# A ring of seven places for the second weight matrix, an earlier read of partial results, and a third inverse class in sixteen frequency classes

## The chip, the cores and the metric

The kernel runs on one core of one Trainium2 chip. Time is device microseconds of one execution. The kernel before takes 1217.4 us (median of three runs, 1216.28 to 1218.68). One of its executions was profiled: it took 1216.67 us, and from its first to its last instruction 1214.9 us.

## The reference

The kernel computes `x + s * g` for `x` of 2048 rows and 1024 columns. `xn` is the layer norm of `x`. `s` is a spectral filter of `xn`: a two-dimensional real Fourier transform, a product with the complex weights `w_r + i w_i`, and the inverse transform. `g` is a feed-forward block with hidden width 3584:

```python
xn = _layernorm(x, axis=-1)
X = rfft2(xn) * (w_r + 1j * w_i)
s = irfft2(X, s=(S, D))
h = silu(xn @ w1)
g = silu(h @ w2)
return x + s * g
```

## The kernel before, in words

**Two streams of work share the engines.** The feed-forward block is the foreground: it gives TensorE (PE in the profile) most of its matmuls. The Fourier transforms are the background: small matmuls that are put between the foreground's, with long chains of additions on VectorE (DVE).

**The second feed-forward matmul** (`h @ w2`) is done as seven products in place of eight, in the manner of Strassen, on sums and differences of blocks. Product `m` (0 to 6) has eight row blocks `j`; I write (4,5) for product 4, row block 5. Each (m,j) is 42 matmuls of 512 columns into one PSUM tile `pb` (lines 563 to 565), in two halves of 21. Each matmul is in half precision, three to one product of 32-bit numbers: high part by high part, high by low, low by high.

**w2 in pieces.** For each product, 14 pieces of w2 (128 by 512) are loaded into a ring of six places (`jr`), by DMAs that GpSimd (POOL) issues (line 421). For products 4 and 5 a piece is the sum of two blocks of w2: a second DMA adds the second block onto the first (line 425, "join"), and must wait until the first has landed. Then ScalarE (ACT) makes the high part (line 244) and VectorE the low part (line 247). `w2_gen` (lines 412 to 464) hands this out in steps: at the step of piece n it issues loads up to n + 5 and joins up to n + 3, and then the high part of piece n. A piece's place in the ring is free when VectorE has made its low part.

**Partial results.** Products 1, 3, 4 and 5 leave partial sums in DRAM (`pd`), through a ring of eight places (`pt`), and products 4 and 6 read them back (`load_parts`, line 552, DMAs of SyncE, SP in the profile). In product 4, VectorE adds the product to both partial results (lines 615 and 616, tiles `pl4_j_1` and `pl4_j_0`); the one is stored again, the other goes through a last chain: SiLU on ScalarE (line 653), the factor from the spectral filter on VectorE (line 641), an accumulating DMA that adds `x` (line 644) and a store (line 645), both issued by GpSimd.

**The inverse transform** goes by four residue classes c of rows, in the order 1, 3, 0, 2. For each class, four groups of matmuls (line 1318, PSUM tile `iu`, groups g = 0 to 3, 48 matmuls each) are followed by additions on VectorE, by `split` (line 1392: `us`, high part on ScalarE, low part on VectorE, line 1395), and then by a second set of matmuls (line 1407, PSUM tile `id`, 48 for each of four parts p), whose every part reads all four `us`. `iu` and `id` share a pool of two PSUM tiles, so the third group waits until VectorE has read the first. There are two forms of the additions: `coarse` (line 1321: eight classes of frequencies, matmuls of 128 columns, 13 VectorE instructions for a group) and `post` (line 1344: sixteen classes, matmuls of 64 columns, 32 VectorE instructions). The tuple `FINE` (line 25) names the classes that use `post`.

**What sets the order.** Nothing is reordered at run time: each engine has one queue in the order in which the program issues. The builder runs through the 56 (m,j); after each half it takes one step of `w2_gen` and as many background steps as its own clock of PE and VectorE allows (`meter` and `work`). More VectorE instructions in a background step therefore move the later background steps to later (m,j). SP's and POOL's DMAs stand in such queues too, and one that waits holds up those behind it.

Of the kernel before, what the change touches and what calls it, by code (L numbers as in the profile page):

```python
# [10 lines left out]
F32 = mybir.dt.float32  # L11
# [10 lines left out]
WARM = [38, 8, 0, 0, 8, 0, 0, 0]  # L22
LEAD, PAUSE, LAST, EARLY = 1.0, -1, 6, 2
IORDER = (1, 3, 0, 2)
FINE = (1, 3)
DIRECT = tuple((6, j) for j in range(8))
SUMMED = (4, 5)
TURNED = (2, 3)
# [88 lines left out]
def spectral_ffn(ctx, tc, x, w_r, w_i, w1, w2, ca, kc, ci, tw, pm, out):  # L117
# [15 lines left out]
    H = {"p": hstack.enter_context(tc.tile_pool(name="hid", bufs=1))}  # L133
    pf = ctx.enter_context(tc.tile_pool(name="pf", bufs=4, space=PSUM))
    pt = ctx.enter_context(tc.tile_pool(name="pt", bufs=2, space=PSUM))
# [59 lines left out]
    def tile_of(pool, shape, dtype, name, tag, bufs):  # L195
        while len(held.get(tag, ())) >= bufs - 1:
            d = held[tag][0]
            deferred.remove(d)
            d[1]()
        return pool.tile(shape, dtype, name=name, tag=tag, bufs=bufs)  # L200
# [211 lines left out]
    def w2_gen():  # L412

        todo = [(m, q) for m in range(7) for q in range(NP)]
        raw = {}

        def load(n):
            if n < len(todo):
                m, q = todo[n]
                raw[n] = J["p"].tile([128, 512], F32, name=f"jr{n}", tag="jr", bufs=6)  # L420
                nc.gpsimd.dma_start(raw[n], ws[m][q] if m in ws else w2_block(m, q, 0))  # L421

        def join(n):
            if n < len(todo) and todo[n][0] in SUMMED:
                nc.gpsimd.dma_start(raw[n], w2_block(*todo[n], 1), accum_op=OP.add)

        def split(n):
            m, q = todo[n]
            if q % 7 == 0:
                w2t[m, q // 7] = fp.tile([128, 7, 2, 512], F16, name=f"w2_{m}_{q // 7}", tag="big", bufs=4)  # L430
            high(w2t[m, q // 7][:, q % 7, 0], raw[n], sc2[:, q:q + 1])

        def rest(n):
            m, q = todo[n]
            w = w2t[m, q // 7][:, q % 7]
            low(w[:, 1], raw.pop(n), sc2[:, q:q + 1], w[:, 0])
            ready2[0] = n

        fed = [0, 0]

        def feed(loads, joins):
            while fed[1] < min(joins, fed[0]):
                join(fed[1])
                fed[1] += 1
            while fed[0] < min(loads, len(todo)):
                load(fed[0])
                fed[0] += 1

        feed(4, 0)
        yield 0  # L450
        yield 0
        for n, (m, q) in enumerate(todo):
            while q % 7 == 0 and (done2[0] < m - 1 or chunks[0] <= (3 if m else q // 7) and m < 2):
                if n and ready2[0] < n - 1:
                    rest(n - 1)
                elif n:
                    feed(min(fed[0] + 1, n + 6), n + 6)
                yield 0
            feed(n + 5, n + 3)
            split(n)  # L460
            if n and ready2[0] < n - 1:
                rest(n - 1)
            yield 0.1
        rest(n)
# [87 lines left out]

    def load_parts(m, j):
        for k in READS[m]:
            t_ = tile_of(H["p"], [128, 512], F32, f"pl{m}_{j}_{k}", "pt", 8)
            nc.sync.dma_start(t_, pd[k, j])
            part[k, j] = t_

# [28 lines left out]
    def acc(m, j, ps, cols=slice(0, 512)):  # L587
        tt = nc.vector.tensor_tensor
        g, p = j // 4, j % 4
        ask_rows(m, j)  # L590

        def fresh(name):
            return tile_of(H["p"], [128, 512], F32, f"{name}_{j}", "pt", 8)

        def keep(k, t_):
            store("pt", 2, lambda: nc.sync.dma_start(pd[k, j], t_))

        def evac():
            if m == 0:
                kept[j] = H["p"].tile([128, 512], F32, name=f"kept{j}", tag="kept", bufs=8)  # L600
                nc.scalar.activation(kept[j], ps, AF.Copy)
            elif m == 1:
                t_ = fresh("c11")
                tt(t_, kept[j], ps, op=OP.subtract)
                keep(0, t_)
            elif m == 2:
                tt(kept[j], kept[j], ps, op=OP.add)
            elif m == 3:
                t_ = fresh("c21")
                nc.scalar.activation(t_, ps, AF.Copy)  # L610
                tt(kept[j], kept[j], ps, op=OP.subtract)
                keep(1, t_)
            elif m == 4:
                t_, u = part.pop((1, j)), part.pop((0, j))
                tt(t_, t_, ps, op=OP.add)
                tt(u, u, ps, op=OP.add)
                keep(0, u)
                return final(2 * g + 1, p, 0, t_)
            elif m == 5:
                t_ = fresh("c12")  # L620
                nc.scalar.activation(t_, ps, AF.Copy)
                tt(kept[j], kept[j], ps, op=OP.add)
                keep(2, t_)
                return final(2 * g + 1, p, 1, kept.pop(j))
            else:
                t_, u = part[2, j][:, cols], part[0, j][:, cols]
                tt(t_, t_, ps, op=OP.subtract)  # L627
                tt(u, u, ps, op=OP.add)
                a_, b_ = final(2 * g, p, 1, t_, cols), final(2 * g, p, 0, u, cols)

                def both():
                    x_, y_ = a_(), b_()
                    return (lambda: (x_ and x_(), y_ and y_(), None)[2]) if x_ or y_ else None

                return both

        return evac
# [27 lines left out]
    A = {}  # L665
# [322 lines left out]
    def open_f():  # L988
        J["p"] = ctx.enter_context(tc.tile_pool(name="jit", bufs=1, side="right"))
        J["i"] = ctx.enter_context(tc.tile_pool(name="fi", bufs=1, side="right"))  # L990
        B["es"] = ExitStack()
        B["p"] = B["es"].enter_context(tc.tile_pool(name="flt", bufs=1, side="right"))
        B["k"], B["v"], B["w"], B["z"] = {}, {}, {}, {}
        B["a"] = J["i"].tile([128, 8192], F16, name="kv", tag="a", bufs=1)
        A["junk"] = J["p"].tile([128, 512], F32, name="junk", tag="jr", bufs=6).bitcast(mybir.dt.bfloat16)

    def f_gen():
        bp = B["p"]
# [298 lines left out]
    def i_gen(c):  # L1297
# [10 lines left out]
        def mat(g):  # L1308
            n_ = 2 if c in FINE else 1
            ps = pt.tile([128, 2, n_, 4, 2, 64 // n_], F32, name=f"iu{c}_{g}", tag="ft")  # L1310
# [210 lines left out]
    with tc.manual_schedule():  # L1521
# [49 lines left out]
        J = {}  # L1571
# [90 lines left out]
        for n, (m, j) in enumerate(seq):  # L1662
# [16 lines left out]
            for k in range(2):  # L1679
                while ready2[0] < m * NP + 7 * k + 6:  # L1680
                    slot(wq)
                if m == 6 and j and k == 0:
                    load_parts(m, j)
                mm2(m, j, ps, k)
                if k == 0:
                    settle()
                    if m < 6 or j == 0:
                        load_parts(m, j)
                    tick()
                    work()  # L1690
# [41 lines left out]
```

## Time and profile before

| What | us |
|---|---|
| median of three runs | 1217.4 |
| the profiled execution | 1216.67 |
| its span, first to last instruction | 1214.9 |
| TensorE matmuls, busy | 1199.7 (99%) |
| VectorE busy | 1024.9 (84%) |
| ScalarE busy | 519.3 (43%) |
| GpSimd busy | 319.6 (26%) |
| moved by DMA | 304.31 MB, 250 GB/s in the mean |

In a timeline row the columns are: start in us from the span's start, length in us, engine, line, operation, out<-in, shapes, count; in brackets the idle time of that engine before it and what ended it. Rows of one kind that follow each other are merged, with a count. `pb`, `iu`, `id`, `jr`, `us` are the tiles named above; the profile leaves out their numbers. A share of busy time is a mean over stages: what a change is worth is read in its own stage, here the last two products but two (about 950 to 1130 us).

### The profile page before, as it was taken

To read this page: it belongs to the slowest core of one execution; us is meant where nothing else is said; L and a number is where in the kernel's file an instruction comes from. 1 tells how busy PE (TensorE), PEld (TensorE's weight loads), DVE (VectorE), ACT (ScalarE), POOL (GpSimd) and SP (SyncE) were. 2 spreads that over 40 slices of the span, in tenths; PEclk is the share of its full clock that TensorE was granted. 3 is DMA by queue.
4 is the path that set the end of the run, shared out by engine and by line. 5 is a ranking of instruction groups with operands and counts; after the bars stand their busy time and mean duration, and the time that the engine had idled before them with its cause. 6 is when DMAs were issued, how large, how long until landed. Compare 5 with 4: busy or idle time off the path is not lost.

```text
span 1214.9 us, 21954 instructions
## 1 busy us (share of the span) xinstructions
PE 1199.7 (99%) x8362; PEld 596.3 (49%) x8362; DVE 1024.9 (84%) x2196; ACT 519.3 (43%) x713; POOL 319.6 (26%) x491
## 2 busy tenths in 40 slices
PE   8999999999999999999999999999999998999998
PEld 5544455445445544544444455444454444554545
DVE  7578889999988999589969999966897896979855
ACT  5874556768557656353624222221222223233112
POOL 2240133334222222233322334620222223221000
PEclk9999999999999999999999999999999999999999
DMA  7478657679589886859898998995988999898798
GB/s 245 135 156 203 186 193 259 198 250 342 161 293 301 270 300 197 256 144 246 253 286 243 253 294 251 242 269 184 220 252 258 259 318 335 268 330 270 244 349 309
DMA packets 166186, 304.31 MB, mean 250 GB/s; under 512 B 31600, under 2 KB 84752, under 8 KB 166080
## 3 DMA queue, kind: packets, MB, share of 16 engines
q1 hardware_dynamic: 125344, 175.61, 46.6%
q0 software_dynamic: 40448, 127.16, 36.3%
q8 instruction: 65, 1.06, 0.3%
q14 instruction: 41, 0.34, 0.1%
q10 hardware_dynamic: 288, 0.13, 0.0%
HBM read 185.92 MB, written 112.74 MB: 246 GB/s over the span
## 4 chain that ended last, share of the span: by engine, by line
PE 89%; DVE 5%; DMA 2%; ACT 2%; issue 1%; POOL 0%; SPq 0%; DVEq 0%; ACTq 0%; POOLq 0%
PE pa L479 44%; PE pb L563 13%; PE pb L565 13%; PE pb L564 13%; PE fx L1034 2%; DMA jr<-in_B_w_dram 2%; PE id L1407 2%; PE iu L1318 1%; ACT xp L742 1%; DMA x<-in_A_x_dram 1%; PE fa L822 1%; PE fa L823 1%; PE fa L824 1%; PE tp L757 0%; DVE w L247 0%
## 5 line engine op out<-in xcount | busy, mean ns | idle before, releaser
L479 PE MATMUL pa<-xnT,w 128*128 128x512 f16 x2688 | 585.5, 379 | 2.3 <-DVE xnT L766 1.1
L479 PEld LDWEIGHTS <-w 128*128 128x128 f16 x2688 | 262.0, 98 | 313.4 <-ACT w L244 3.1
L563 PE MATMUL pb<-w,ht 128*128 128x512 f16 (+2 forms) x812 | 301.0, 372 | 0.0
L564 PE MATMUL pb<-w,ht 128*128 128x512 f16 (+2 forms) x812 | 300.4, 372 | 0.0
L565 PE MATMUL pb<-w,ht 128*128 128x512 f16 (+2 forms) x812 | 300.3, 372 | 0.0
L565 PEld LDWEIGHTS <-ht 128*128 128x128 f16 x812 | 79.5, 98 | 91.3 <-issue 0.3
L563 PEld LDWEIGHTS <-ht 128*128 128x128 f16 x812 | 79.4, 98 | 90.3 <-issue 0.2
L564 PEld LDWEIGHTS <-ht 128*128 128x128 f16 x812 | 79.5, 98 | 87.1
L495 ACT ACTIVATE h<-pa,s 128x512 f32<-128x512 f32 x112 | 75.4, 677 | 62.9 <-PE pa L479 59.0
L244 ACT ACTIVATE w<-jr,sc 128x512 f16<-128x512 f32 x98 | 67.7, 712 | 48.4 <-DMA jr<-in_B_w_dram 30.5
L244 ACT ACTIVATE hosum<-hr,hs 128x1536 f16<-128x1536 f32 x28 | 44.1, 1574 | 97.0 <-DVE hr L524 71.8
L247 DVE SCALAR_TENSOR_TENSOR w<-jr,sc,w 128x512 f16<-128x512 f32 x98 | 71.6, 745 | 3.2 <-ACT w L244 3.2
L517 POOL DMA_DIRECT2D hd_sum<-hosum x26 | 26.1, 1004 | 174.0 <-DVE hosum L247 110.8
L247 DVE SCALAR_TENSOR_TENSOR hoone<-h,hs,hoone 128x2048 f16<-128x2048 f32 x28 | 65.6, 2344 | 6.5 <-ACT hoone L244 6.4
L421 POOL DMA_DIRECT2D jr<-in_B_w_dram x56 | 41.8, 752 | 89.4 <-ACT us L1394 27.8
L244 ACT ACTIVATE hoone<-h,hs 128x2048 f16<-128x2048 f32 x28 | 55.9, 1997 | 15.7 <-DMA hd_one<-hoone 9.1
L247 DVE SCALAR_TENSOR_TENSOR hosum<-hr,hs,hosum 128x1536 f16<-128x1536 f32 x28 | 50.7, 1810 | 5.8 <-ACT hosum L244 5.8
L517 POOL DMA_DIRECT2D hd_one<-hoone x26 | 29.4, 1133 | 88.3 <-DVE hoone L247 56.5
L653 ACT ACTIVATE pl<-pl,c 128x512 f32<-128x512 f32 (+2 forms) x28 | 17.6, 655 | 75.9 <-DVE pl L627 52.3
L523 DVE TENSOR_TENSOR hr<-h 128x1024 f32<-128x1024 f32 x28 | 34.1, 1219 | 17.8 <-ACT h L495 17.6
L244 ACT ACTIVATE w<-w1r,rs 128x1024 f16<-128x1024 f32 x28 | 32.0, 1143 | 38.6 <-DVE w L247 17.4
L1394 ACT ACTIVATE us<-uu 128x1024 f16<-128x1024 f32 x16 | 16.8, 1053 | 62.1 <-DVE uu L234 62.1
(265 smaller groups left out, 1722.3 us busy)
## 6 DMA issues: line engine op xcount, KB each, us to landing
ht<-hd_one SPq DMA_DIRECT2D x64, 448.0 KB, 7.6
hd_one<-hoone POOLq DMA_DIRECT2D x26, 1024.0 KB, 7.6
ht<-hd_sum SPq DMA_DIRECT2D x48, 448.0 KB, 6.3
jr<-in_B_w_dram POOLq DMA_DIRECT2D x84, 256.0 KB, 7.2
hd_sum<-hosum POOLq DMA_DIRECT2D x26, 768.0 KB, 5.7
w1r<-in_B_w_dram SPq DMA_DIRECT2D x28, 512.0 KB, 7.3
w2m<-in_B_w_dram SPq DMA_DIRECT2D x28, 512.0 KB, 6.1
ws<-scr POOLq DMA_DIRECT2D x42, 256.0 KB, 6.2
```

The source lines that it names most:

```text
L244: nc.scalar.activation(hi, raw, AF.Copy, scale=scale)
L247: nc.vector.scalar_tensor_tensor(lo, raw, scale, hi, op0=OP.mult, op1=OP.subtract)
L421: nc.gpsimd.dma_start(raw[n], ws[m][q] if m in ws else w2_block(m, q, 0))
L479: nc.tensor.matmul(ps, w[:, wh, d], xt[:, xh, d], start=(n == 0), stop=(n == 23))
L495: nc.scalar.activation(h32[q, g][:, 2 * (c % 2) + f % 2], ps, AF.Silu, scale=s1[:, f:f + 1])
L517: defer(1, lambda: stores[0].dma_start(hall[names, g][:, :, :, q].rearrange("f k p h s -> f k p (h s)"), o.rearrange("f k p h s -> f k p ( ...
L523: tt(sums[:, 0:2], hq[:, 0::2], hq[:, 1::2], op=OP.subtract)
L563: nc.tensor.matmul(ps, hh[:, 0], w[:, 0], start=first, stop=False)
L564: nc.tensor.matmul(ps, hh[:, 0], w[:, 1], start=False, stop=False)
L565: nc.tensor.matmul(ps, hh[:, 1], w[:, 0], start=False, stop=last)
L1034: nc.tensor.matmul(o, k[rows_, h, e + 2 * x, kh, kind], B["v"][u, h][rows_, e + 2 * x, vh, cols], start=(n == 0 and kind == 1), stop=(n == ...
L1407: nc.tensor.matmul(ps[:, half, g], us[g][rows_, uh, 2 * p + r], C["ci"][rows_, ch, g, r], start=(n == 0 and r == 0), stop=(n == 2 and r == 1))
```

## The change

Three edits, and what follows from them in the sizes of the rings.

1. The ring of w2 pieces has seven places in place of six; at the step of piece n, loads go up to n + 6 and joins up to n + 4.
2. In product 4 the partial results of (4,1) to (4,7) are asked for ahead of the first half's matmuls, as product 6 did already, and not behind them. The ring of partial results gives one place up: seven in place of eight.
3. Class 0, the third of the inverse transform, uses `post` (sixteen classes) in place of `coarse`.

```diff
-FINE = (1, 3)
+FINE = (1, 3, 0)
...
         def load(n):
             if n < len(todo):
                 m, q = todo[n]
-                raw[n] = J["p"].tile([128, 512], F32, name=f"jr{n}", tag="jr", bufs=6)
+                raw[n] = J["p"].tile([128, 512], F32, name=f"jr{n}", tag="jr", bufs=7)
                 nc.gpsimd.dma_start(raw[n], ws[m][q] if m in ws else w2_block(m, q, 0))
...
                 elif n:
-                    feed(min(fed[0] + 1, n + 6), n + 6)
+                    feed(min(fed[0] + 1, n + 7), n + 7)
                 yield 0
-            feed(n + 5, n + 3)
+            feed(n + 6, n + 4)
             split(n)
...
     def load_parts(m, j):
         for k in READS[m]:
-            t_ = tile_of(H["p"], [128, 512], F32, f"pl{m}_{j}_{k}", "pt", 8)
+            t_ = tile_of(H["p"], [128, 512], F32, f"pl{m}_{j}_{k}", "pt", 7)
...
         def fresh(name):
-            return tile_of(H["p"], [128, 512], F32, f"{name}_{j}", "pt", 8)
+            return tile_of(H["p"], [128, 512], F32, f"{name}_{j}", "pt", 7)
...
-                if m == 6 and j and k == 0:
+                if m in (4, 6) and j and k == 0:
                     load_parts(m, j)
                 mm2(m, j, ps, k)
                 if k == 0:
                     settle()
-                    if m < 6 or j == 0:
+                    if m < 4 or m == 5 or j == 0:
                         load_parts(m, j)
```

What this does to the order of the engines' queues is shown at three places. The first is PE, at the third group of class 0 (`iu0_2`); `ht4_5_0` and `ht4_5_1` are the two halves of the operand of (4,5). Before:

```order
L565 LDWEIGHTS ht4_5_0_11178
L565 MATMUL pb4_5_11440<-w2_4_0_9522,ht4_5_0_11178 128x512
L1318 LDWEIGHTS zt0_10704
L1318 MATMUL iu0_2_11475<-tables_8768,zt0_10704 128x128
```

And with the change:

```order
L565 LDWEIGHTS ht4_5_1_11183
L565 MATMUL pb4_5_11462<-w2_4_1_10052,ht4_5_1_11183 128x512
L1318 LDWEIGHTS zt0_10707
L1318 MATMUL iu0_2_11526<-tables_8770,zt0_10707 128x64
```

The third group stood behind the first half of (4,5) and now stands behind the whole of it, and it has 64 columns in place of 128. The first two groups stand where they stood, ahead of (4,5). The fourth group moves from behind (4,5) to behind (4,6), the `id` matmuls of class 0 from the middle of (5,0) and of (5,1) to the middle of (5,2) and of (5,3), the `iu` matmuls of class 2 from behind (5,3) to behind (5,5), and its `id` matmuls from the middle of (5,7) to behind (6,0).

The second place is POOL's queue at the first accumulating DMA of the last chain (`pl4_0_1`). Before:

```order
L425 DMA jr76_10733<-in_B_w_dram 128x512
L421 DMA jr78_11003<-in_B_w_dram 128x512
L644 DMA pl4_0_1_10696<-in_A_x_dram 128x512
L425 DMA jr77_10897<-in_B_w_dram 128x512
L421 DMA jr79_11118<-in_B_w_dram 128x512
L425 DMA jr78_11003<-in_B_w_dram 128x512
L421 DMA jr80_11148<-in_B_w_dram 128x512
L644 DMA pl4_1_1_10891<-in_A_x_dram 128x512
```

And with the change:

```order
L425 DMA jr76_10703<-in_B_w_dram 128x512
L421 DMA jr78_10900<-in_B_w_dram 128x512
L425 DMA jr77_10736<-in_B_w_dram 128x512
L421 DMA jr79_11006<-in_B_w_dram 128x512
L644 DMA pl4_0_1_10699<-in_A_x_dram 128x512
L425 DMA jr78_10900<-in_B_w_dram 128x512
L421 DMA jr80_11121<-in_B_w_dram 128x512
L425 DMA jr79_11006<-in_B_w_dram 128x512
L421 DMA jr81_11151<-in_B_w_dram 128x512
L644 DMA pl4_1_1_10871<-in_A_x_dram 128x512
```

One pair, the join of piece 77 and the load of piece 79, has moved ahead of the accumulating DMA; behind it each join and load is one piece further on.

The third place is VectorE at the end of the additions for the last group of class 0 (`uu0_3`), up to the low part of that group (`us0_3`), which the `id` matmuls of class 0 read. Before:

```order
L234 TENSOR_TENSOR uu0_3_11723<-ub0_3_11713 128x2x128
L641 SCALAR_TENSOR_TENSOR pl4_5_1_11466<-fs3_1_0_11565,s_sc_209,pl4_5_1_11466 128x512
L615 TENSOR_TENSOR pl4_6_1_11673<-pl4_6_1_11673,pb4_6_11647 128x512
L616 TENSOR_TENSOR pl4_6_0_11675<-pl4_6_0_11675,pb4_6_11647 128x512
L1395 SCALAR_TENSOR_TENSOR us0_3_11792<-uu0_3_11723,us0_3_11792 128x1024
```

And with the change:

```order
L234 TENSOR_TENSOR uu0_3_11899<-ub0_3_11870 128x2x128
L247 SCALAR_TENSOR_TENSOR w2_6_0_11829<-jr85_11320,sc2_219,w2_6_0_11829 128x512
L641 SCALAR_TENSOR_TENSOR pl4_7_1_11772<-fs3_3_0_11824,s_sc_209,pl4_7_1_11772 128x512
L622 TENSOR_TENSOR kept0_6696<-kept0_6696,pb5_0_11835 128x512
L247 SCALAR_TENSOR_TENSOR w2_6_0_11829<-jr86_11492,sc2_219,w2_6_0_11829 128x512
L247 SCALAR_TENSOR_TENSOR w2_6_0_11829<-jr87_11522,sc2_219,w2_6_0_11829 128x512
L1395 SCALAR_TENSOR_TENSOR us0_3_11999<-uu0_3_11899,us0_3_11999 128x1024
```

The low part of the last group stood behind the results of (4,6); now it stands behind those of (4,7) and (5,0) and behind four pieces of product 6.

More of the change, by code (lines that the diff above doesn't have):

```diff
@@ L994, in open_f @@
         B["a"] = J["i"].tile([128, 8192], F16, name="kv", tag="a", bufs=1)
-        A["junk"] = J["p"].tile([128, 512], F32, name="junk", tag="jr", bufs=6).bitcast(mybir.dt.bfloat16)
+        A["junk"] = J["p"].tile([128, 512], F32, name="junk", tag="jr", bufs=7).bitcast(mybir.dt.bfloat16)
     def f_gen():
```

## The prediction

> **What bounds the kernel now.** I read the page first (busy times, chain of waits), then the waits of TensorE alone, then the timelines of one engine after the other back from the place that these named. These three rows are from the page's busy times, its chain, and the view of PE's waits:
>
> ```profile
> PE 1199.7 (99%) x8362; PEld 596.3 (49%) x8362; DVE 1024.9 (84%) x2196; ACT 519.3 (43%) x713; POOL 319.6 (26%) x491
> PE 89%; DVE 5%; DMA 2%; ACT 2%; issue 1%; POOL 0%; SPq 0%; DVEq 0%; ACTq 0%; POOLq 0%
> PE iu L1318 <- DVE uw L1329: 4.0, 2, 2.4
> ```
>
> TensorE is the bound: any matmul time that is saved, and any gap that closes, comes off the end, and any gap that opens is added. Its largest wait is 4.0 us in two gaps, at the inverse transform's first matmuls. PE's timeline has the places:
>
> ```profile
> 980.68 0.39 PE L563 MATMUL pb<-w,ht 128*128 128x512 f16 x1
> ...
> 1007.98 2.85 PE L1318 MATMUL iu<-tables,zt 64*128 64x128 f16 x96
> ...
> 1017.08 1.51 PE L1318 MATMUL iu<-tables,zt 64*128 64x128 f16 x48 [1.61 <-DVE uw L1329]
> ...
> 1025.66 2.74 PE L1318 MATMUL iu<-tables,zt 64*128 64x128 f16 x48 [2.42 <-DVE uw L1329]
> ```
>
> These are the four groups of class 0, the first two together. The third and fourth each wait until VectorE has read an older group out of PSUM. The fourth also takes 2.74 us for what took 1.51. The view by stages tells why (after the name: length, PE, PEld, DVE, ACT and POOL busy with counts, granted clock, DMA share, GB/s):
>
> ```profile
> 1025.60:1028.50 2.90, 2.84 (x49) 2.61 (x50) 2.80 (x10) 0.00 (x0) 0.00 (x0) 0.50 1.08 300
> ```
>
> After the two gaps the clock is granted by half. The Trainium skill ("TensorE: Matmul & The Clock Gate", What's actually happening) has the clock halved after an idle window of about 3.4 us. By that rule, gaps of 1.61 and 2.42 us would cost no clock, and the change would gain 1.5 us less than I sum up; the row shows the half clock without such a gap, and the row decides.
>
> Why was VectorE late? It waited for ScalarE's copy (line 1325), and ScalarE's timeline has that copy behind pieces of w2:
>
> ```profile
> 1008.96 0.72 ACT L244 ACTIVATE w<-jr,sc 128x512 f16<-128x512 f32 x1 [5.88 <-DMA jr<-in_B_w_dram]
> 1014.50 0.72 ACT L244 ACTIVATE w<-jr,sc 128x512 f16<-128x512 f32 x1 [4.21 <-DMA jr<-in_B_w_dram]
> 1015.13 0.58 ACT L1325 ACTIVATE uw<-iu 128x512 f32<-128x512 f32 x1
> 1019.53 0.72 ACT L244 ACTIVATE w<-jr,sc 128x512 f16<-128x512 f32 x1 [3.83 <-DMA jr<-in_B_w_dram]
> ...
> 1021.75 0.58 ACT L1325 ACTIVATE uw<-iu 128x512 f32<-128x512 f32 x1
> ```
>
> The first two rows are pieces 79 and 80, the fourth is piece 81. The first group has been ready since about 1009, and its copy stands until 1015.13 behind a piece whose second block had not landed. POOL's timeline has the cause of that:
>
> ```profile
> 976.19 0.56 POOL L421 DMA_DIRECT2D jr<-in_B_w_dram  x1 [3.95 <-ACT w L244]
> 988.75 0.87 POOL L644 DMA_DIRECT2D pl<-in_A_x_dram  x1 [12.00 <-DVE pl L641]
> 989.30 1.22 POOL L425 DMA_DIRECT2D jr<-in_B_w_dram  x1
> ...
> 1001.02 0.86 POOL L425 DMA_DIRECT2D jr<-in_B_w_dram  x1 [2.45 <-issue]
> ...
> 1003.88 0.90 POOL L425 DMA_DIRECT2D jr<-in_B_w_dram  x1 [0.87 <-DMA jr<-in_B_w_dram]
> ```
>
> For 12 us the queue was held by an accumulating DMA that waited for VectorE, with the join of piece 77 behind it (989.30). The joins of 79 and 80 follow at 1001.02 and 1003.88.
>
> **The change part by part: the ring and the order of PE.** With the pair that moves ahead of the first accumulating DMA, each later place in POOL's queue carries the next piece. So the join of piece 80 stands where that of 79 stood, about 1001, and if its landing is as quick, ScalarE makes its high part at 1008.96 and the copy of the first group ends at 1010.2, not 1015.7. On PE the third group now comes after the whole of (4,5). A product takes (1007.98 - 980.68) / 3 = 9.10 us, so with the new group times (below) the third group is wanted at 1007.98 + 1.50 + 9.10 = 1018.6 and the fourth at 1028.5. VectorE reads the first group out by 1011.5, and even from the old start at 1015.74 by 1017.1. For the second I take its chain below: 1024. Both gaps close, one by the order alone: 4.03 us.
>
> **Class 0 in sixteen classes, on PE.** The view of groups by shape over all four classes has, on line 1318:
>
> ```profile
> L1318 PE MATMUL iu<-tables,zt 64*128 64x128 f16 x384 | 13.0, 228 | 4.0 <-DVE uw L1329 4.0
> L1318 PE MATMUL iu<-tables,zt 64*128 64x64 f16 x384 | 6.6, 190 | 0.0
> ```
>
> Two classes each; and in the timeline, one sixteen-class pair and group (class 3), then an undisturbed eight-class pair and group (class 2):
>
> ```profile
> 916.96 1.57 PE L1318 MATMUL iu<-tables,zt 64*128 64x64 f16 x96
> ...
> 927.64 0.87 PE L1318 MATMUL iu<-tables,zt 64*128 64x64 f16 x48
> ...
> 1089.04 2.85 PE L1318 MATMUL iu<-tables,zt 64*128 64x128 f16 x96
> ...
> 1096.47 1.51 PE L1318 MATMUL iu<-tables,zt 64*128 64x128 f16 x48
> ```
>
> A class costs 1.57 + 2 x 0.87 = 3.31 us with 64 columns and 2.85 + 2 x 1.51 = 5.87 us with 128: 2.56 us less. Class 0 itself took 2.85 + 1.51 + 2.74 = 7.10; the 1.23 us above 5.87 are the half clock, and the first matmuls of the product behind it give about 0.2 more. So 3.8 + 0.2 = 4.0 us. Here the Trainium skill speaks against the change: the same page (Wait - 56ns, not 53.3ns?) has matmuls never start closer together than about 25 ns however few columns they have. By that, 48 would take 1.20 us and not 0.87, and the four groups would give back some 1.5 us of the 2.56 (an estimate). But 0.87 us for 48 is 18 ns each, on this line with this shape, so the trace does not bear it out here.
>
> Sum on PE: 4.03 + 4.0 = **8.0 us** less, if no new wait comes.
>
> **What sixteen classes cost VectorE.** These are VectorE's timeline at a group of class 3 (first two rows: start of its additions, and of the next instruction) and of class 0:
>
> ```profile
> 918.56 0.69 DVE L1350 TENSOR_TENSOR uw<-iu,uw 128x512 f32<-128x512 f32 x1 [7.61 <-ACT uw L1348]
> ...
> 926.38 0.68 DVE L611 TENSOR_TENSOR kept<-kept,pb 128x512 f32<-128x512 f32 x1
> ...
> 1015.74 0.69 DVE L1328 TENSOR_TENSOR uw<-iu,uw 128x512 f32<-128x512 f32 x1 [5.27 <-ACT uw L1325]
> ...
> 1020.66 0.75 DVE L641 SCALAR_TENSOR_TENSOR pl<-fs,s_sc,pl 128x512 f32<-128x512 f32 x1
> 1021.33 0.68 DVE L615 TENSOR_TENSOR pl<-pl,pb 128x512 f32<-128x512 f32 x1
> 1021.92 0.68 DVE L616 TENSOR_TENSOR pl<-pl,pb 128x512 f32<-128x512 f32 x1
> 1022.52 0.74 DVE L247 SCALAR_TENSOR_TENSOR w<-jr,sc,w 128x512 f16<-128x512 f32 x1
> 1023.18 1.22 DVE L1395 SCALAR_TENSOR_TENSOR us<-uu,us 128x1024 f16<-128x1024 f32 x1
> 1024.32 0.68 DVE L1328 TENSOR_TENSOR uw<-iu,uw 128x512 f32<-128x512 f32 x1
> ```
>
> From start to start, a group takes 7.82 us in sixteen classes and 4.92 in eight: 4 x 2.90 = 11.6 us more for VectorE. What has to cover this is the new place of the `id` matmuls. PE wants the first of them after 5.5 products and two groups: 1007.98 + 1.50 + 5.5 x 9.10 + 2 x 0.80 = 1061.1, and the low part of the last group three quarters into its 48, 1062.2. In the new order VectorE has, from the first group's start to that low part: 4 groups (31.3), line 641 five times (0.67 each, 3.35), lines 615 and 616 four times (0.59 + 0.60, 4.8), eight pieces of w2 (0.66, 5.3), four low parts (1.14, 4.6) and one line 622 (as 615, 0.6): 49.9 us. From 1010.2 this ends at 1060.1, if it never waits. It reads the second group out after 7.82 + 0.67 + 1.19 + 1.32 + 1.14 + 1.3 = 13.4 us, at 1023.6, as used above.
>
> It will wait a little. Bounds: below, nothing. Above, 4 us: twice about 0.5 for ScalarE's turn before a low part, and for (4,5) the partial result that SP asks for late. Its rows, SP's timeline and then the landing times (least, median, most) of the store issued at 1011.48 and of the two `ht` loads issued at 1023:
>
> ```profile
> 1012.63 2.54 SPq L556 DMA_DIRECT2D pl<-pd  x2
> ...
> 1023.04 0.96 SPq L544 DMA_DIRECT2D ht<-hd_one  x2
> ...
> DMA to landing us min/median/max: 10.4/10.4/10.4
> ...
> DMA to landing us min/median/max: 10.3/10.7/11.1
> ```
>
> In the ring of eight, the two loads for (4,5) waited for the store of `pl4_0_1`; in the ring of seven the second waits, by the new program, for the store of `pl4_1_1`. Its place in POOL's queue is no earlier (the piece taken out ahead comes back behind), so it lands at 1011.48 + 10.4 = 1021.9, and the load behind it, at 12 us, near 1034. VectorE would be there at 1032: up to 2 us. Then the end is 1061 to 1064 against 1062.2. Beside it, SP issues the `ht` loads for (5,2) after VectorE's line 616 of (4,6): 1010.2 + 34.0 (three groups and what lies between) + 1 to 3 = 1045 to 1047; at 10.7 us they land from 1056 to 1058, and (5,2) starts at 1056.5. These two overlap (a PE that waits at the one is later at the other). I take **1.5 us**, the middle of 0 and 3.
>
> The earlier request in product 4 moves no DMA past another in SP's order; it only frees the request from standing behind VectorE's turn in the builder. I cost it at nothing, since VectorE and PE cover it. The other loads that move (products 0 to 3) stand where PE has no wait at all in the view of its waits: nothing, bounded above by the cover of three free `pb` tiles, 27 us.
>
> **Forecast.** The profiled execution's 1216.67 lies 0.7 under the median, so the median counts: 1217.4 - 8.0 + 1.5 = **1210.9 us**.
>
> **Rivals.** (a) Nothing new is waited for, VectorE's 49.9 us run through: 1217.4 - 8.0 = 1209.4. For it: class 3 went through the same form with no PE wait. Against it: there VectorE had no lines 641 between.
>
> (b) VectorE becomes the bound of this stage: the loads of (4,3) and (4,5) land some 3 us later than I took, so the last low part comes 3 to 4 us late and the clock is halved once more (3.4 us at half is 1.6): about 1214. For it, a DMA share of 1.08 in the quoted stage.
>
> (c) The ring does not bring piece 80 sooner, because the DMAs are full and not because the queue was held. Then VectorE starts at 1015.74, as before; the order still closes the gaps at the groups, but the last low part comes at 1015.74 + 49.9 + 1.5 = 1067.1, 4.9 us late: with the half clock 1217.4 - 8.0 + 6.5 = 1215.9. The 12.00 us of POOL's wait speak against it.
>
> (d) Slower: the ring of seven for partial results. SP's queue is in order, so the load of (4,5) that waits for a store holds back the `ht` loads for (5,0). PE wants these at 1007.98 + 1.50 + 27.3 + 1.6 = 1038.4, and at 10.7 us they must be issued by 1027.7; from then on each us is PE's. The gain is used up if SP stands there until 1035.7, so if the store lands 14 us later than I worked out. At 1039 the time would be 1221.
>
> **How the numbers follow.** Forecast 0.50, (a) 0.22, (b) 0.13, (c) 0.09, (d) 0.06. A measurement of this kernel can tell about 0.2% from no change, 2.4 us: faster is below 1215.0. Forecast and (a) are faster, of (b) 0.10, of (c) 0.02: 0.84. Within 0.2%: the rest of (b), 0.06 of (c), 0.01 of (d): 0.10. Slower 0.06. The range goes from 1208.3 (full gain and a run 1.1 under the median, as the fastest of the three was) to 1215.0, the upper end of (b).
>
> **What would show it.** PE's waits: no row for line 1318, and the two gaps gone; if they stand, the ring did nothing. Line 1318's 64-column row at 576 matmuls and about 9.9 us, the 128-column row at 192 and 5.8. ScalarE's copy of the first group of class 0 near 1010: if at 1015, (c). A PE wait on line 1407 for VectorE's line 1395 of 0 to 3 us: if above, (b). A PE wait on lines 563 to 565 for `ht` shows SP late, at (5,2) within the forecast, at (5,0) for (d). Granted clock 1 from 1010 to 1070. I am wrong altogether if PE's busy time does not fall, or if the last products lose what the middle ones gain.

## The result, and the profile after

The changed kernel takes **1210.36 us** (median of four runs, 1210.27 to 1210.89), the kernel before 1217.4 us beside it: a ratio of 0.9945, 95% interval 0.9931 to 0.9958. A second set of runs, taken later, gave 1211.27 us against 1216.32, 0.9955 (0.9941 to 0.9969). The forecast was 1210.9. The number came out right; one of its terms did not exist, and a cost that I had not foreseen stood in its place.

The page's busy times and chain, and then the largest row of PE's waits, of the changed kernel (its profiled execution took 1210.39 us, its span 1208.6):

```profile
PE 1196.1 (99%) x8362; PEld 592.9 (49%) x8362; DVE 1035.7 (86%) x2272; ACT 518.5 (43%) x713; POOL 320.4 (27%) x491
PE 86%; DVE 7%; ACT 3%; DMA 2%; issue 1%; POOL 0%; SPq 0%; DVEq 0%; ACTq 0%; POOLq 0%
```

```profile
PE tp L757 <- ACT x L742: 2.0, 3, 1.1
```

PE's busy time fell by 3.6 us, VectorE's rose by 10.8, and the wait at line 1318, the largest before, is gone from the list. PE's timeline at class 0, and then the view of groups by shape, line 1318:

```profile
1008.14 1.57 PE L1318 MATMUL iu<-tables,zt 64*128 64x64 f16 x96
1018.81 0.87 PE L1318 MATMUL iu<-tables,zt 64*128 64x64 f16 x48
1028.79 0.87 PE L1318 MATMUL iu<-tables,zt 64*128 64x64 f16 x48
```

```profile
L1318 PE MATMUL iu<-tables,zt 64*128 64x64 f16 x576 | 10.0, 190 | 0.0
L1318 PE MATMUL iu<-tables,zt 64*128 64x128 f16 x192 | 5.9, 216 | 0.0
```

The groups start 0.2 and 0.3 us from where they were forecast (1018.6 and 1028.5), with no gap ahead of them. The view by stages has the clock granted in full there (third figure from the end):

```profile
1023.00:1031.00 8.00, 8.00 (x83) 3.91 (x81) 7.83 (x33) 0.72 (x1) 0.00 (x0) 1.00 1.05 374
```

ScalarE's timeline shows the copy of the first group right behind piece 80:

```profile
1008.75 0.72 ACT L244 ACTIVATE w<-jr,sc 128x512 f16<-128x512 f32 x1 [5.05 <-DMA jr<-in_B_w_dram]
1009.37 0.58 ACT L1348 ACTIVATE uw<-iu 128x512 f32<-128x512 f32 x1
```

Now the end. These are rows of the timeline of the kernel before: VectorE's last additions, and the start of PE's last group of matmuls between them:

```profile
1205.44 0.42 DVE L627 TENSOR_TENSOR pl<-pl,pb 128x256 f32<-128x256 f32 x1 [0.24 <-PE pb L565]
...
1206.44 0.48 DVE L641 SCALAR_TENSOR_TENSOR pl<-fs,s_sc,pl 128x256 f32<-128x256 f32 x1 [0.24 <-ACT pl L653]
...
1207.59 0.22 PE L563 MATMUL pb<-w,ht 128*128 128x128 f16 x1
...
1211.86 0.29 DVE L647 TENSOR_TENSOR pl<-pl,fx 128x128 f32<-128x128 f32 x1
```

And the same rows of the changed kernel:

```profile
1197.42 0.42 DVE L627 TENSOR_TENSOR pl<-pl,pb 128x256 f32<-128x256 f32 x1 [0.24 <-DMA fx<-in_A_x_dram]
...
1199.57 0.22 PE L563 MATMUL pb<-w,ht 128*128 128x128 f16 x1
1199.60 0.48 DVE L641 SCALAR_TENSOR_TENSOR pl<-fs,s_sc,pl 128x256 f32<-128x256 f32 x1 [1.42 <-DMA fs<-sd]
...
1205.60 0.29 DVE L647 TENSOR_TENSOR pl<-pl,fx 128x128 f32<-128x128 f32 x1
```

From the first `iu` group of class 0 to PE's last group it took 199.61 us before (1007.98 to 1207.59) and takes 191.43 now: **8.2 us less**, against a sum of 8.0. But from the start of that last group to VectorE's last addition it took 4.27 us and takes 6.03. I call this time the end of a kernel. VectorE now waits for the rows of the last product (`fs`, `fx`), 1.42 us for the first of them: **1.8 us are lost at the end**. 8.2 - 1.8 = 6.4; the profiled executions differ by 6.28.

Why are these rows late? SP's timelines, before and then changed, have its request for the first of them:

```profile
1199.03 0.32 SPq L577 DMA_DIRECT2D fs<-sd  x1
```

```profile
1193.17 0.43 SPq L577 DMA_DIRECT2D fs<-sd  x1
```

SP asked 8.6 us ahead of PE's last group before, and asks 6.4 us ahead of it now; the load then took 5.2 us to land before, and takes 6.3. Against that group the row lands 3.3 us later: 2.2 by the later request, 1.1 by the slower landing. Further up, SP's timeline of the changed kernel has a stand, and the view of SP's waits from 1122 to 1160, behind it, names what it stands for:

```profile
1128.28 0.94 SPq L556 DMA_DIRECT2D pl<-pd  x2
1140.45 0.32 SPq L1454 DMA_DIRECT2D sd<-s  x1
...
1141.35 0.72 SPq L577 DMA_DIRECT2D fx<-in_A_x_dram  x1
1148.40 0.32 SPq L577 DMA_DIRECT2D fs<-sd  x1
```

```profile
SPq L1454 <- DVE s L1444: 11.1, 1, 11.1
SPq L577 <- DMA out_dram<-kept: 8.5, 2, 6.2
```

It stands 11.1 us at the store of the first result of class 2, which VectorE has not finished, and then 6.2 us for a place of the ring `kept`. The kernel before stood nearly as long at that store, but earlier against the end; its waits in the same window have

```profile
SPq L1454 <- DVE s L1444: 17.6, 4, 9.9
```

The view by stages shows the hole that this leaves in the DMAs (last three columns: granted clock, DMA share, GB/s). Before, and then changed:

```profile
1122.00:1132.00 10.00, 10.00 (x131) 5.82 (x130) 7.05 (x17) 3.35 (x5) 2.87 (x4) 1.00 0.61 160
1132.00:1142.00 10.00, 10.00 (x130) 5.64 (x129) 9.86 (x31) 1.91 (x4) 0.45 (x1) 1.00 0.63 219
...
1202.00:1210.00 8.00, 8.00 (x116) 7.58 (x113) 6.84 (x17) 2.51 (x6) 0.00 (x0) 1.00 0.83 299
```

```profile
1134.00:1144.00 10.00, 10.00 (x126) 5.63 (x121) 9.27 (x28) 2.49 (x4) 1.45 (x2) 1.00 0.45 130
1144.00:1154.00 10.00, 10.00 (x88) 5.08 (x87) 9.83 (x35) 0.60 (x1) 0.56 (x1) 1.00 0.68 191
...
1194.00:1202.00 8.00, 8.00 (x116) 7.57 (x113) 5.47 (x12) 1.81 (x4) 0.00 (x0) 1.00 1.02 377
```

The hole ended 66 us ahead of PE's last group before (1207.6 - 1142) and ends 46 us ahead of it now. Behind the hole the share is now 1.00 to 1.05 in every stage to the end; before, the last stage had come down to 0.83. So the first theory after the result, **L**: sixteen classes for class 0 push the `id` matmuls of class 2 behind (6,0), where they were in (5,7); SP's queue stands there later, and the rows of the last products come late. Its rival, **D**: the DMAs are simply too full for a PE that is 8 us quicker, wherever class 2 stands. Beside it stood the prediction's own question, whether the ring or the new order of PE had given the gain: **A**, the ring is needed; **B**, the order alone does it.

### The profile page after: what moved, and what is told of

It is laid out like the page before. It is cut to its first block, busy times and chain, and to the rows that moved or that the text cites. A ratio compares the mean times of both kernels' runs of the same rounds, so it can differ in the third digit from the quotient of the medians.

```text
span 1208.6 us, 22019 instructions
## 1 busy us (share of the span) xinstructions
PE 1196.1 (99%) x8362; PEld 592.9 (49%) x8362; DVE 1035.7 (86%) x2272; ACT 518.5 (43%) x713; POOL 320.4 (27%) x491
## 3 DMA queue, kind: packets, MB, share of 16 engines
q8 instruction: 65, 1.06, 0.4%
## 4 chain that ended last, share of the span: by engine, by line
PE 86%; DVE 7%; ACT 3%; DMA 2%; issue 1%; POOL 0%; SPq 0%; DVEq 0%; ACTq 0%; POOLq 0%
PE pa L479 38%; PE pb L563 14%; PE pb L564 14%; PE pb L565 14%; PE fx L1034 2%; PE id L1407 2%; PE iu L1318 1%; DVE hoone L247 1%; ACT xp L742 1%; DMA vd<-Rs 1%; DMA fx<-in_A_x_dram 1%; DMA x<-in_A_x_dram 1%; DMA hd_one<-hoone 0%; ACT w L244 0%; PE fa L822 0%
## 5 line engine op out<-in xcount | busy, mean ns | idle before, releaser
L517 POOL DMA_DIRECT2D hd_one<-hoone x26 | 29.5, 1134 | 87.5 <-DVE hoone L247 55.7
```

The costliest lines, as they stand in the source:

```text
L517: defer(1, lambda: stores[0].dma_start(hall[names, g][:, :, :, q].rearrange("f k p h s -> f k p (h s)"), o.rearrange("f k p h s -> f k p ( ...
```

## The experiments

**Sixteen classes alone.** The kernel before with

```diff
-FINE = (1, 3)
+FINE = (1, 3, 0)
```

> Before with one edit, class 0 in sixteen classes; rings and loads as before. Theory A (POOL's held queue is what makes the copy late, and the ring is what frees it): the copy of the first group of class 0 still ends near 1015.7, the two gaps at line 1318 close by the new order alone, but the low part before the first id matmuls comes some 5 us late with a stretch of half clock behind it, a PE wait on line 1407 for line 1395, 1214 to 1216 us. Theory B (the new order of PE alone gives the gain and the ring nothing): no PE wait on line 1407, 1210 to 1211 us. If the loss at the end (1.8 us after the last matmul in the changed kernel) comes from class 2's id standing one and a half products later, it shows here too, unless PE is itself late by then.

Measured: 1217.24 us, ratio to before 1.0008 (0.9995 to 1.002). No gain: A. Rows of ScalarE and PE in its timeline, and then of the view by stages, show where it went:

```profile
1016.25 0.72 ACT L244 ACTIVATE w<-jr,sc 128x512 f16<-128x512 f32 x1 [3.89 <-DMA jr<-in_B_w_dram]
1016.88 0.58 ACT L1348 ACTIVATE uw<-iu 128x512 f32<-128x512 f32 x1
...
1068.10 0.40 PE L1407 MATMUL id<-tables,us 64*128 64x128 f16 x8 [2.79 <-ACT us L1394]
1069.36 2.95 PE L1407 MATMUL id<-tables,us 64*128 64x128 f16 x52 [0.86 <-DVE us L1395]
```

```profile
1069.30:1072.20 2.90, 2.85 (x52) 2.69 (x52) 2.90 (x5) 1.93 (x3) 1.45 (x2) 0.50 1.04 226
```

The copy still stands behind a piece of w2 and starts 6.8 us after the first group does (1010.04), where in the changed kernel it is 1.2; VectorE's chain of four groups starts as much later, and the two gaps at line 1318 come back as two gaps at line 1407, with the half clock behind them. 0.72 us at line 1318 are left. It ends 1.2 to 3.2 us above the 1214 to 1216 that I expected, since the loss at the end is there too: its end is 6.75 us, though PE is only 2 us quicker than before from class 0 to its last group (1010.04 to 1207.59). That speaks for L and against D, but weakly: the profiled execution took 1.9 us more than the median. The kernel without the ring, below, has the same order and the same place of class 2, with PE 1.2 us quicker than before; there the end is 4.9 us.

**Everything but the sixteen classes.** The changed kernel with `FINE = (1, 3)`.

> The changed kernel with class 0 back in eight classes, so the ring of seven, the loads a turn sooner, the ring of seven partial results and their earlier request alone; PE's order is that of before. Theory A: the copy of the first group ends near 1010, both gaps at line 1318 close and with them the half clock (4.03 + about 1.4 us), and id of class 2 stands where it stood, so that the end after the last matmul is as before (about 4.8 us by the page's last rows): 1212.0 us. Theory B: the gaps stand, 1216 to 1217.5. If the DMAs are simply too full for a PE that is quicker, whatever the place of class 2, some 1.2 us of the 5.4 are lost at the end: 1213.2.

Measured: 1211.41 us, ratio 0.9967 (0.9955 to 0.9979). Both gaps are closed with the order of before, and the half clock went with them: the stage from 1023 to 1031, first below, has a granted clock of 1.00. Behind it the two rows of the timeline that give the end:

```profile
1023.00:1031.00 8.00, 8.00 (x79) 4.31 (x80) 7.40 (x19) 2.15 (x3) 0.00 (x0) 1.00 1.05 371
```

```profile
1203.41 0.22 PE L563 MATMUL pb<-w,ht 128*128 128x128 f16 x1
...
1207.69 0.29 DVE L647 TENSOR_TENSOR pl<-pl,fx 128x128 f32<-128x128 f32 x1
```

PE takes 194.0 us from class 0 to its last group (from 1009.42), 5.6 less than before, and the end is 4.28 us: nothing is lost there, though PE is 5.6 us quicker. That is against D as it stands. L again, and A: the ring gives 5.6 of the 8.2 us.

**Without the earlier request.** The changed kernel with the last hunk of the diff undone.

> The changed kernel without the earlier request of partial results in product 4 (both rings and sixteen classes stay). By the prediction, which costs that edit at nothing: 1210.4 us, as the changed kernel, within 0.3. Rival: the earlier request is what keeps VectorE's line 615 fed, and without it the low part before id comes 2 us or more late: 1212 to 1213, with a PE wait on line 1407.

Measured: 1211.0 us, ratio 0.9961 (0.9948 to 0.9973), within the spread of the changed kernel's two results: nothing, as the prediction costed it. In its profile the operand of (5,5) came 1.6 us late; that is one execution, and its cause was not followed.

**Without the ring.**

```diff
-tag="jr", bufs=7
+tag="jr", bufs=6
-                    feed(min(fed[0] + 1, n + 7), n + 7)
+                    feed(min(fed[0] + 1, n + 6), n + 6)
-            feed(n + 6, n + 4)
+            feed(n + 5, n + 3)
```

> The changed kernel with the ring of w2 pieces back at six and its loads at their old turn; sixteen classes, the earlier request and the ring of seven partial results stay. Theory A: as the kernel with sixteen classes alone, 1214 to 1216, with the copy of the first group at 1015 and a PE wait on line 1407. Theory B: 1210.4.

Measured: 1216.19 us, ratio 0.9998 (0.9989 to 1.0008): as with the sixteen classes alone. In the profile PE waits 2.48 and 0.65 us at line 1407, and the copy of the first group starts at 1014.52. A is settled: neither the order nor the earlier request gives anything without the ring.

**Class 2 late, and nothing else.** The kernel without the sixteen classes, with class 2 held back until its matmuls stand where the changed kernel has them:

```diff
-        for _ in range(1 if c == IORDER[0] else 2):
+        for _ in range(1 if c == IORDER[0] else 6 if c == IORDER[-1] else 2):
             yield PAUSE
```

> The kernel with both rings and the earlier request but eight classes for class 0 (its last result 1211.4 us), with four turns of waiting ahead of class 2, so that the matmuls iu and id of class 2 stand where the changed kernel has them (id after the first product of 6, not in the last of 5). PE's own work is unchanged. Theory L (the late id of class 2 holds SP's queue at its store, and the loads of the last rows come late): DVE's last instruction ends 1.5 to 2.5 us later after PE's last group than the 4.3 us that it had, 1213 to 1214 us. Theory D (the DMAs are too full at the end for a PE that is quicker, wherever class 2 stands): the end as it was, 1211.4.

Measured: 1213.46 us, ratio 0.998 (0.997 to 0.9991), 2 us above the kernel without this edit, though the intervals of the two ratios overlap. In its profile (an execution of 1211.77 us, 1.7 under the median) the hole and the wait are back, in the view by stages and in VectorE's timeline:

```profile
1136.00:1146.00 10.00, 10.00 (x130) 5.71 (x125) 9.16 (x27) 2.53 (x4) 1.45 (x2) 1.00 0.40 119
...
1196.00:1204.00 8.00, 8.00 (x117) 7.64 (x114) 6.14 (x13) 2.40 (x6) 0.00 (x0) 1.00 1.00 374
```

```profile
1200.83 0.48 DVE L641 SCALAR_TENSOR_TENSOR pl<-fs,s_sc,pl 128x256 f32<-128x256 f32 x1 [0.31 <-DMA fs<-sd]
```

Its end is 5.29 us and not 4.28. PE takes the same 194.0 us. SP asks for the first of the last rows 6.1 us ahead of PE's last group, where without this edit it was 8.3. So in these two profiles the place of class 2 costs 1.0 us by itself; I had expected 1.5 to 2.5.

**The last rows on another queue.** The changed kernel, with the loads of rows for the last product on POOL's queue:

```diff
-            nc.sync.dma_start(t_[-1], src[:, hsl])
+            (nc.gpsimd if (c, p) == (2, 3) else nc.sync).dma_start(t_[-1], src[:, hsl])
```

> The changed kernel with the four loads of rows for the last product asked on POOL's queue, which is empty by then, and not on SP's. Theory L (these loads stand behind some 10 others in SP's in-order queue): they land before VectorE wants them, its waits for them go, and the end comes 4.3 us after PE's last group begins and not 6.0: 1208.6 us. Theory D (the DMA engines are full; a transfer asked elsewhere lands no sooner, or another is late in its place): 1210.4.

Measured: 1213.49 us, ratio 0.9975 (0.9965 to 0.9984): no gain, and by the medians 2 to 3 us slower than the changed kernel. VectorE no longer waits for the last product's rows; it waits for those of the product ahead:

```profile
1197.36 0.75 DVE L641 SCALAR_TENSOR_TENSOR pl<-fs,s_sc,pl 128x512 f32<-128x512 f32 x1 [1.12 <-DMA fs<-sd]
1199.87 0.69 DVE L647 TENSOR_TENSOR pl<-pl,fx 128x512 f32<-128x512 f32 x1 [1.75 <-DMA fx<-in_A_x_dram]
```

So L in the form in which I had it (loads behind others in SP's queue) falls here. The last rows were asked 9.6 us ahead of PE's last group, in place of 6.4, but took 6.0 to 8.3 us to land, in place of 6.3 to 6.8. The rows of the product ahead were asked when they had been, from 1188.6 on, and took 6.4 (`fs`) and 7.8 us (`fx`) in the median, in place of 5.3 and 5.4. What is asked elsewhere takes its time from what is under way: the engines are full, as D has it. What is left of L is the hole.

**The stores of class 2 on another queue.**

```diff
-                sstore[c, p] = lambda: nc.sync.dma_start(sd[c, p], sf)
+                sstore[c, p] = lambda: (nc.gpsimd if c == IORDER[-1] else nc.sync).dma_start(sd[c, p], sf)
```

> The changed kernel with the four stores of class 2's results (line 1454) on POOL's queue, so that SP does not stand for 11 us at the first of them. If that stand alone makes the last loads late, the end comes back to 4.3 us: 1208.6 us. If SP then stands as long at the next loads, which take the place of the kept rows of (5,6) and (5,7), nothing changes: 1210.4. POOL stands at the stores in its place, with the accumulating DMAs of those kept rows behind it: if these are what counts, slower, 1212 or more.

Measured: 1212.97 us, ratio 0.9971 (0.996 to 0.9983); its end is 7.19 us. SP's waits from 1114 to 1160:

```profile
SPq L577 <- DMA out_dram<-kept: 17.7, 3, 9.9
...
SPq L577 <- DVE pl L641: 6.3, 1, 6.3
```

SP does not stand at line 1454 any more. It stands at the next loads instead, 17.7 us for places of kept rows and 6.3 for VectorE's line 641, 24 us in all, and the hole grows: the DMA share is 0.46, 0.50 and 0.87 in the three stages from 1134 to 1164, where the changed kernel has 0.45, 0.68 and 1.00. The last rows are asked only 4.3 us ahead of PE's last group. So taking the store out of SP's queue does not set SP free. It is slower, as I had expected for the case that the accumulating DMAs of the kept rows, now behind the stores on POOL's queue, are what counts; whether this is the reason was not followed.

**Sixteen classes for class 2 in place of class 0** (`FINE = (1, 3, 2)` in the changed kernel).

> The changed kernel with sixteen classes for class 2 in place of class 0. PE's own work is as in the changed kernel (2.56 us less than with eight), the copy of class 0 is in time by the ring, and id of class 2 stands after the first product of 6, as in the changed kernel. Theory L: its end loses about as much as there: 1210.4, within 0.7. Theory D: as much too, as PE is as quick. If the loss came from VectorE's longer chain of class 0 alone, the end is as before the change: 1208.8.

Measured: 1211.16 us, ratio 0.9963 (0.9951 to 0.9975), with an end of 6.51 us in its profile (an execution of 1214.62 us, 3.5 above the median, in which PE also waited 0.8 us at line 1407). The order of PE puts `id` of class 2 behind (6,0) here too. The median, which is that of the changed kernel and not 1208.8, speaks for a loss without a longer chain of class 0. It does not tell L from D.

**Class 2 half a product sooner.** To the changed kernel, ahead of the last yield of the class's generator:

```diff
+            if c == IORDER[2] and p == 4:
+                lead[0] = 4.0
-            yield 3.4 if p else 0.3
+            yield PAUSE if c == IORDER[-1] and p else 3.4 if p else 0.3
```

> The changed kernel with class 2 let run ahead by half a product: iu from the middle of (5,5), id from the middle of (6,0), a turn between one id group and the next. Theory L (SP's queue stands until the first result of class 2, the DMAs have a hole there, and the end pays since they are full from then on): the hole ends 3 to 4.5 us sooner and the loss at the end shrinks from 1.8 to about 0.5. But VectorE has 5.8 us of waiting for the store of class 0 ahead of class 2, so its last low part before id comes 1 to 2 us after PE wants it, a new PE wait on line 1407: 1210 to 1211 in all, no gain.

> The same, with the stores of class 0's results (line 1454) on POOL's queue as well, so that VectorE does not wait 5.8 us for the first of them (18 us from issue to landing on SP's queue in the changed kernel). Theory L: no PE wait on line 1407, the hole of the DMAs ends 4 us sooner, the loss at the end goes: 1208.7 us. If the store lands no sooner on POOL's queue, as the kernel beside it: 1210 to 1211. If POOL, standing at a store, holds the joins of w2's pieces back: a PE wait on lines 563 to 565 for line 244, 1212 or more.

Measured: 1211.2 us for the first (0.9954, 0.9939 to 0.9969) and 1211.67 for the second (0.9957, 0.9939 to 0.9974), with 1211.27 for the changed kernel beside them, for which this was written:

> The changed kernel itself once more, beside the next two. 1210.4 us as before if its time does not depend on the chip; if the waits of VectorE at the end for loads vary with the chip, 1210 to 1213, with DVE's waits for rows in its last 20 us and nowhere else.

No gain that can be told. In the first, the store of class 2's first result goes out at 1136.74 (1141.60 in the changed kernel beside it), the DMA share from 1135 to 1145 is 0.83 where it was 0.42, and the end is 4.96 us in its profile against 5.33: the right way, and too little to measure. The PE wait that was expected at line 1407 did not come. In the second, PE waited 0.6 us at line 1407 and the end was 7.47 us. The expectation of 1208.7 was wrong, and why was not followed. That the ends of the changed kernel's two profiles are 6.03 and 5.33 shows how far this wait varies from one execution to the next; its runs beside these went from 1209.0 to 1212.9.

**Less to move.** The last test takes bytes away and leaves every DMA at its place:

```diff
-        store(tag, 1, lambda: queue.dma_start(outs[4 * c + p][:, first:first + cols.stop - cols.start], o))
+        n_ = 128 if c == 0 else cols.stop - cols.start
+        store(tag, 1, lambda: queue.dma_start(outs[4 * c + p][:, first:first + n_], o[:, 0:n_]))
```

> The changed kernel with the eight stores of the output rows of (6,0) to (6,3) (line 649) cut to their first 128 of 512 columns: the same DMAs at the same places of SP's queue, but 1.5 MB less, which at the 390 GB/s of that stage is 3.9 us of transfer time. It leaves three quarters of those output rows unwritten. Theory L, in the form that the last runs left (after the hole at the late id of class 2 the DMA engines are full to the end, and what comes last is late by what is left over): VectorE's waits for the rows of the last product go, the end comes 7.3 us after PE's last group begins, as in the kernel before, and not 8.3 to 9.0: 1208.6 to 1209.5 us. Rival (SP's order and its pace of issuing make the loads late, not the bytes): the waits stay, 1210.4 to 1211.3.

Measured: 1209.13 us, ratio 0.9951 (0.9936 to 0.9967); the profiled execution 1208.6. The hole is as it was (first row, by stages), and VectorE's waits for rows are gone (its timeline):

```profile
1133.00:1143.00 10.00, 10.00 (x154) 6.15 (x149) 8.39 (x24) 2.53 (x4) 1.45 (x2) 1.00 0.43 124
```

```profile
1198.33 0.49 DVE L641 SCALAR_TENSOR_TENSOR pl<-fs,s_sc,pl 128x256 f32<-128x256 f32 x1 [0.24 <-ACT pl L654]
...
1203.76 0.29 DVE L647 TENSOR_TENSOR pl<-pl,fx 128x128 f32<-128x128 f32 x1
```

PE's last group starts at 1199.48, so the end is 4.28 us, that of the kernel before. This is one execution, and the times do not show a gain: the ratio to the kernel before beside it, which took 1215.44 us here, lies between the changed kernel's two, 0.9945 and 0.9955.

The profile also says how the bytes act. SP asked for the first of the last rows at 1191.16, 8.3 us ahead of PE's last group in place of 6.4, and the load took 5.7 us to land in place of 6.3. So most of what came back came by an earlier request. Only bytes were taken away and the order of SP's queue is the same, so in this profile SP's pace behind the hole hangs on the bytes ahead of it; L and its rival had set bytes and pace against each other. Over the profiles that keep these loads on SP's queue, the end follows the request: 4.28 us where it came 8.3 to 8.6 us ahead of PE's last group, 4.9 to 6.8 where it came 5.8 to 6.9 ahead, and 7.2 to 7.5 where it came 4.3 to 4.5 ahead.

## Why the prediction was right

**The bound and the gaps: right.** PE was the bound; both gaps closed, and the half clock with them. The 0.72 us left in the kernel with the sixteen classes alone show that the order by itself closes one gap and most of the other (the prediction gave it one), only to hand the wait on to line 1407.

**The ring: right.** ScalarE made the high part of piece 80 at 1008.75, where the prediction had 1008.96, and VectorE started its additions at 1009.98, for 1010.2. POOL was still held for 12.00 us; the joins behind it were only one piece further on. Rival (c), in which the ring does nothing, came true as to the time in the kernel without it: 1216.19 us, for the 1215.9 that (c) gave. Its reason, full DMAs, is not what that kernel shows, and its PE wait was 3.1 us at line 1407, not 4.9.

**Class 0 on PE: right.** 1.57 + 2 x 0.87 = 3.31 us in place of 7.10, with 48 matmuls of 64 columns in 0.87 us, as class 3 had them. The sum for PE was 8.0, and 8.2 were measured.

**The new wait of 1.5 us: wrong, it was 0.** PE has no row for line 1407 in its waits. The timeline has VectorE's low part of the last group, SP's turn at the two loads for (4,5) and at those of `ht` for (5,2):

```profile
1011.08 10.45 SPq L556 DMA_DIRECT2D pl<-pd  x2
...
1044.97 1.40 SPq L544 DMA_DIRECT2D ht<-hd_one  x2
...
1060.56 1.23 DVE L1395 SCALAR_TENSOR_TENSOR us<-uu,us 128x1024 f16<-128x1024 f32 x1 [1.02 <-ACT us L1394]
```

and the DMA view has how long the second load for (4,5) and the two for (5,2) took to land, asked for each of the two windows apart:

```profile
pl<-pd SPq DMA_DIRECT2D x1, 256.0 KB, 8.1
```

```profile
ht<-hd_one SPq DMA_DIRECT2D x2, 448.0 KB, 7.3
```

The low part ended at 1061.8, within the 1061 to 1064 of the prediction and ahead of the 1062.2 at which it had PE want it; PE began these `id` matmuls at 1061.43, without a gap. VectorE's 49.9 us of work became 51.8 from its start at 1010.0: 1.9 us more, about half of the bound of 4. The other half was mis-sized landing times. SP stood 10.45 us at the second load for (4,5) until the store ahead had landed, to within 0.7 us as forecast (1021.2 for 1021.9), but the load then took 8.1 us and not 12, and was there ahead of VectorE. The loads for (5,2) were issued at 1045, as forecast, and took 7.3 us in the median, not 10.7. I had taken both from the kernel before: 10.7 from two `ht` loads, 12 from the loads for (4,5), which took 13.4 and 12.3 us there. How full the DMAs are does not explain the difference. The load for (4,5) landed at a DMA share of 1.06 (1021 to 1030), and in the changed kernel the pairs of `ht` loads issued at 1010.1, 1022.6, 1032.8, 1045.0 and 1047.5 took 14.2, 9.5, 7.0, 7.3 and 13.1 us in the median, at shares of 0.97 to 1.08. What sets a landing time stays open.

**The loss at the end: not in the sum.** The prediction said that it would be wrong "if the last products lose what the middle ones gain". They lost 1.8 of 8.2 us. The step that failed is the part on sixteen classes: I worked out what the new place of the `id` matmuls of class 0 would be covered by, and did not ask the same of class 2, which the same edit moves by one and a half products. The rows that would have told were there in the profile of before: SP's stand at the store of class 2, and behind the hole 60 us with a DMA share of 0.98 to 1.05 and then 0.83 in the last 8, a slack of about 1.4 us. The share alone would not have told, since without the sixteen classes PE is 5.6 us quicker, the last stage still has 0.81, and nothing is lost. The two errors, 1.5 us that did not come and 1.8 that I had not seen, cancelled. The start was luck too: the 66 later runs of the kernel before, in four sets, have medians of 1215.44 to 1216.41 and not 1217.4, so the gain is 7.0 us in the first set of the changed kernel and about 5 in the second, for a forecast of 6.5. That the median was met to 0.5 us is in part luck.

**What each part is worth.** The ring with its sooner loads gives 5.6 us on PE and 4 to 5 in time. Sixteen classes for class 0 give 2.6 us more on PE and lose 1 to 1.8 of it at the end, in two profiles. What is left in time is not resolved: 1211.41 without, 1210.36 and 1211.27 with, and the intervals of the ratios overlap. Without the ring they give nothing. The earlier request gives nothing that can be measured. No version that was tried beats the changed kernel by more than the measurement can tell.

## What to carry to other kernels

When an edit moves one piece of background work, list everything that the same clock moves behind it, and look for what each of them releases: here a store at which an in-order queue stands, and from there the bytes that are still to be moved. Read the DMA share backwards from the end, and beside it how far ahead of the last matmuls the last loads are asked. Where the share was full to the end here, asking on another queue only changed which load was late, while taking bytes away brought the request forward. Take no landing time from one neighbouring pair of loads: five pairs of one size took 7.0 to 14.2 us within 40 us.

## What was not expected of the hardware

Loads moved ahead onto an empty queue cost more than they saved: with the last rows on POOL's queue the end went from 6.03 to 7.67 us, at a DMA share of 1.00 to 1.04 up to 1194.

In the kernel with the sixteen classes alone the half clock came after gaps of 2.79 and 0.86 us with 0.40 us of matmuls between them, and in the kernel before after 1.61 and 2.42 us with 6.2 us of matmuls between. The Trainium skill ("TensorE: Matmul & The Clock Gate", What's actually happening) has one idle window of about 3.4 us as the cause. The first pair could be read as such a window with a little work in it; the second cannot, so the measurement stands against the rule there.

In the changed kernel the store of the first result of class 0, issued on SP's queue at 1069.75, landed 18.2 us later, where the first two of class 2, between 1134 and 1154, took 3.4 us in the median. VectorE waited 5.8 us for that one landing; PE shows no wait behind it.
